# One more step of a linear-attention kernel sends its query and key transposes to the DMA engines

## The chip, the cores and the metric

The kernel runs on one core of a Trainium2 chip. The metric is the device time of one execution in microseconds (us). A core has a matrix engine (TensorE, called PE in the profile; its weight loads are PEld), VectorE (DVE), ScalarE (ACT), GpSimd (POOL), a queue that only issues transfers (SyncE, SP) and 16 DMA engines that move the data. [...]

## The reference

Decayed linear attention over 4 batches, 8 heads, 768 tokens and head width 64, in blocks of 64 tokens with a running state, and then a two-layer feed-forward net on its output (3072 tokens, 512 to 2048 to 512, tanh GELU between the layers):

```python
for b in range(nb):                                   # blocks of 64 tokens
    intra = (qb @ kb.T * Dmask) @ vb                  # decay mask, causal
    inter = (qb * lam_pow) @ kv_state
    out[:, :, sl] = intra + inter
    kv_state = lam_block * kv_state + (kb * rev_pow).T @ vb
x = out.transpose(0, 2, 1, 3).reshape(B * S, H * D)
g = gelu_tanh(x @ w_in)
result = g @ w_out
```

Inputs and the result are float32.

## The kernel before, in words

**Steps.** The attention is cut into 24 steps. A step is one run of 256 tokens and one half of the heads (4 heads): step s is token run s // 2, half s % 2. For each step the kernel

- loads q, k and v of the step, three transfers of 256 KB each (`load_step`, L60; the transfers are issued at L70 on the SP queue);
- scales q by a decay into float16 on DVE (`cast_q`, L282), casts k on ACT (`cast_k`, L295) and scales v on POOL (`scale_v`, L266);
- transposes q and k so that the head width lies on the partitions. Steps 0 to 7 do it on PE, eight 128x128 products with the identity (`stage_t`, L321), and then DVE or ACT copies the result out of PSUM (L325 to L330; for step 7 it is DVE, L330). Steps from `FIRST_DMA_T` = 8 on do it by one DMA transpose from SBUF to SBUF (`transpose_dma`, L303), and `stage_t` returns at once;
- computes the scores S (`scores`, L350), masks them on DVE (`causal`, L360), and computes the key-value product (L385), the masked scores times v (L399) and the state times q (L408) into the two banks OK; ACT copies the attention out as xT (`x_out`, L487); DVE updates the state (`update`, L506) and POOL spreads it into u (L513).

From step 13 on, two steps are joined in a `burst` (L415), in which the same products stand at L350, L436, L450 and L461.

**Dense product.** The feed-forward net is cut into seven groups of tokens. Its work waits as a list of pieces (`filler`); `fill(n)` puts the next n pieces on PE. A piece of the first layer (`mm1`) is a run of products at L561, whose bank of PSUM ACT then empties with a GELU (L565). Pieces of the second layer are the products at L576 and L640. The last two groups use a scheme with fewer products (L739).

**What sets the order.** Nothing is scheduled at run time. `pin` keeps every instruction in program order on its engine, and the lower part of the kernel (L922 to L1124) writes the order out by hand: `R(n, s)` is the scores of step n together with the products of step s, `U(n)` the second state update, `prep(n)` the casts, the transpose and the scaling of step n, and `fill` the dense pieces between them. Loads are issued ahead of their use, at the places where the order says so. All of them, the stores and the DMA transposes stand in the one SP queue.

**Buffers.** All PSUM tiles come from one pool of eight banks, handed out in turn: the ninth tile takes the bank of the first, and PE waits until that one has been emptied. In the stretch that matters later the turn is: six first-layer tiles (call them a to f), two score tiles for step 13, two for step 14, then two O tiles and two K tiles of the burst. So the scores of step 14 take the banks of a and b, O those of c and d, and K those of e and f.

**Around the change.** `prep(7)` stands after `U(5)`, `stage_t(7)` after `prep(8)`. At L1011 step 7's scores come two dense pieces after its PE transpose; the casts of step 9 are queued between the scores and the products (`ahead`). `load_step(10)` is split: its v is issued after the transpose of step 9.

Of the kernel before, what the change touches and what calls it, by code (L numbers as in the profile page):

```python
# [15 lines left out]
def kernel(  # L16
# [19 lines left out]
    NF = DFF // P  # L36
    NC = DM // P
    NSTEP = B * NSB * 2
    FIRST_DMA_T = 8
    PSUM = bass.MemoryType.PSUM  # L40

    const = ctx.enter_context(tc.tile_pool(name="const", bufs=1))
# [17 lines left out]
    def load_step(s, names="qkv"):  # L60
        b, r = divmod(s, 2 * NSB)
        sb, half = divmod(r, 2)
        ts = ld32.setdefault(s, [])
        for nm, src in (("q", q), ("k", k), ("v", v)):
            if nm not in names:
                continue
            t = ld.tile([P, HH, 2, D], FP32, tag=nm + "32", name=f"{nm}32_{s}")
            rows = src[b, half * HH : (half + 1) * HH, sb * SB : (sb + 1) * SB, :]
            queue = nc.scalar if (nm, s) == ("v", 0) else nc.sync
            pin(queue.dma_start(out=t[:].rearrange("p h j d -> p h (j d)"),  # L70
                                in_=rows.rearrange("h (p j) d -> p h (j d)", j=2)))
            ts.append(t)
# [97 lines left out]
    def load_ahead(s):  # L170
        if s < NSTEP:
            load_step(s)
# [83 lines left out]
    def prep_v(s):  # L256
        scale_v(s)
        if s >= 6:
            if s + 3 == FIRST_DMA_T + 2:
                load_step(s + 3, "qk")  # L260
            else:
                load_ahead(s + 3)

    def scale_v(s):
        tv = a16p.tile([P, 2, HH, D], FP16, tag="v16", name=f"v16_{s}")
        pin(nc.gpsimd.tensor_tensor(wide(tv[:]), ld32[s][2][:], decay(dv, s), ALU.mult))  # L266
        a16[s] = a16[s] + (tv,)

    def prep_qk(s):
        cast_qk(s)  # L270
        transpose_dma(s)

    def cast_qk(s):
        cast_q(s)
        cast_k(s)
# [23 lines left out]
    def transpose_dma(s):  # L299
        tqk = whole_qk.pop(s)  # L300
        if s >= FIRST_DMA_T:
            o = qkp.tile([P, 2, 2, 2, P], FP16, tag="qkT", name=f"qkT_{s}")
            pin(nc.sync.dma_start_transpose(out=o[:].rearrange("p a j h t -> p (a j h) t"),  # L303
                                            in_=tqk[:].rearrange("p a j h d -> p (a j h d)")))
            qkT[s] = o
            if s == FIRST_DMA_T + 1:
                load_step(s + 1, "v")

    def stage_t(s):
        if s >= FIRST_DMA_T:  # L310
            return
        tq, tk = a16[s][:2]
        if s < 4:
            Tps = [ps_M.tile([P, 2, 2, P], FP16, tag="M", name=f"Tps{i}") for i in range(2)]
        else:
            Tps = ps_M.tile([P, 2, 2, 2, P], FP16, tag="M", name="Tps")
        for i, t in enumerate((tq, tk)):
            to = Tps[i] if s < 4 else Tps[:, i]
            for hp in range(2):
                for j in range(2):  # L320
                    pin(nc.tensor.transpose(to[:, j, hp, :], t[:, j, 2 * hp : 2 * hp + 2, :],  # L321
                                            ident[:]))
        o = qkp.tile([P, 2, 2, 2, P], FP16, tag="qkT", name=f"qkT_{s}")
        if s < 4:
            pin(nc.scalar.activation(out=o[:, 0], in_=Tps[0][:], func=AF.Copy))  # L325
            pin(nc.vector.tensor_copy(out=o[:, 1], in_=Tps[1][:]))
        elif s in (5, 6, 8):
            pin(nc.scalar.activation(out=o[:], in_=Tps[:], func=AF.Copy))
        else:
            pin(nc.vector.tensor_copy(out=o[:], in_=Tps[:]))  # L330
        qkT[s] = o
# [212 lines left out]
    def queue_group(g, lead=0, per_set=0):  # L544
# [71 lines left out]
        def product(m, p, part=None):  # L616

            st = of_group

            def bank(name):  # L620
                if name not in st:
                    st[name] = ps_M.tile([P, 1 if name == "X" else NP, HE], FP32, tag="M",
                                         name="M" + name[0])
                return st[name]

            if m in (2, 5, 3):
                dst = bank("Y" if m in (5, 3) else "W")[:, p]
            else:
                dst = bank(f"X{p}")[:, 0]
            opens = m == 1 or (m in (2, 5) and p == 0)  # L630
            closes = m in (2, 3, 4)
            a, b = FACTORS[m]
            for i in range(HF) if part is None else range(HF // 2 * part, HF // 2 * part + HF // 2):
                lhsT = g_rows(a, i)[:, p * P : p * P + P]
                if b in W_SUMS:
                    rhs = w_sum16[:, w_slot[b], i, :]
                else:
                    F, E = b
                    rhs = w_out16[:, F * HF + i, E * HE : E * HE + HE]
                pin(nc.tensor.matmul(dst, lhsT, rhs, start=(opens and i == 0),  # L640
                                     stop=(closes and i == HF - 1), skip_group_check=True))
            if part == 0:
                return
            last = p == NP - 1

            def temp(name):
                if name not in st:
                    st[name] = mtp.tile([P, NP, HE], FP32, tag=name, name=name)
                return st[name]

            def out_tile(T):
                if f"o{T}" not in st:
                    st[f"o{T}"] = otp.tile([P, NP, 2, HE], FP32, tag="o32", name=f"o{T}")
                return st[f"o{T}"]

            def copy(to, of):
                pin(nc.scalar.activation(out=to, in_=of, func=AF.Copy))  # L657

            def store(T, ps=slice(0, NP), es=slice(0, 2)):
                r = row0 + T * HN  # L660
                rows = out[r : r + HN, :].rearrange("(p q) (e d) -> q p e d", q=P, e=2)
                o = out_tile(T)

                def send():
                    for i in [slice(i, i + 1) for i in range(ps.start, ps.stop)]:
                        pin(nc.sync.dma_start(out=rows[:, i, es], in_=o[:, i, es, :]))

                if g == 2:
                    kept_stores.append(send)
                else:  # L670
                    send()

            one = slice(p, p + 1)
            if m == 1:
                copy(temp("m1")[:, p], dst)
            elif m == 2 and last:
                pin(nc.vector.tensor_tensor(out_tile(0)[:, :, 0, :], st["W"][:], st["m1"][:], ALU.add))
            elif m == 5 and last:
                copy(temp("q")[:], st["Y"][:])
            elif m == 6:  # L680
                copy(temp("u2")[:, p], dst)
            elif m == 3 and last:
                pin(nc.vector.tensor_tensor(out_tile(0)[:, :, 1, :], st["Y"][:], st["u2"][:], ALU.add))
                store(0)
            elif m == 7 and last_group:
                pin(nc.vector.tensor_tensor(out_tile(1)[:, p, 1, :], dst, st["q"][:, p], ALU.add))
                if last:
                    store(1, one, slice(1, 2))
            elif m == 7:
                copy(temp("u3")[:, p], dst)  # L690
                if last:
                    pin(nc.gpsimd.tensor_tensor(out_tile(1)[:, :, 1, :], st["u3"][:], st["q"][:],  # L692
                                                ALU.add))
            elif m == 4:
                copy(out_tile(1)[:, p, 0, :], dst)
                if last_group:
                    store(1, one, slice(0, 1 if last else 2))
                elif last:
                    store(1)
# [198 lines left out]
    def fill(n):  # L898
        for _ in range(min(n, len(filler))):
            filler.pop(0)()  # L900

    def R(n, s, ahead=None, keep=False):

        if n is not None:
            scores(n)
        if ahead:
            ahead()
        products(n, s)
        if n is not None:
            causal(n)  # L910
        if s is not None and s % 2 == 1:
            g, i = group_of[s // 2]
            if i == len(groups[g]) - 1 and g > 0:
                queue_group(g)
        if n is not None and not keep:
            update(n, 0)
# [91 lines left out]
    stage_t(7)  # L1008
    sum_wout(1, 4, DVE)
    fill(2)  # L1010
    R(7, 6, lambda: prep_qk(9))  # L1011
    store_pair(0)
    U(7)
    scale_v(9)
    fill(2)

    FILL = {8: (2, 0, 0, 0), 9: (1, 2, 1, 2), 10: (0, 1, 1, 3), 11: (0, 1, 1, 3), 12: (0, 2, 1, 3)}
    for n, (a, b, c, d) in FILL.items():
# [41 lines left out]
    cast_qk(16)  # L1060
    load_step(17, "qk")
    transpose_dma(16)
    load_step(17, "v")
    while kept_stores:
# [88 lines left out]
```

## Time and profile before

The median is 198.97 us (three runs, 198.95 to 199.12); the profiled execution has a span of 197.1 us on the instructions' own clock.

| engine | busy, us | share of the span |
|---|---|---|
| PE | 191.5 | 97% |
| PEld | 140.0 | 71% |
| DVE | 151.6 | 77% |
| ACT | 122.2 | 62% |
| POOL | 73.3 | 37% |

| transfer | count | median from issue to landing, us |
|---|---|---|
| load of q, k or v, 256 KB | 24 each | 5.1 to 5.4 |
| DMA transpose of q and k of one step | 16 | 5.1 |
| store of 256 KB | 23 | 4.2 |

The page shows busy time, the span in 40 slices of 4.9 us, the chain of work that ended last, and the costliest groups of instructions. In a timeline a line is: start (us from the start of the span), duration, engine, source line, operation, the tiles it writes and reads, its shape, how many are merged; in square brackets the idle time of the engine before it and who ended it. A merged line can hold several instructions. A landing is the moment at which the last of the 16 DMA engines has reported a transfer done; it is the issue time plus the time that the answer on transfers gives for that one issue.

### The profile page before, as it was taken

Reading aid. Unit: us, or ns where it says so; the run is one execution under the profiler, and the core shown is the slowest. Engines: PE = TensorE matmul, PEld = TensorE weight load, DVE = VectorE, ACT = ScalarE, POOL = GpSimd, SP = SyncE. Lnnn points to the kernel's source line nnn. Section 1 sums busy time; section 2 is a strip of 40 time slices with the busy share of each in tenths; the row PEclk is TensorE's granted clock in tenths of the full one; section 3 lists DMA queues with packets and bytes.
Section 4 is the critical chain, followed back from the end, with each engine's and each line's share of the span. In section 5 each row is a group of like instructions: output and inputs, shape, how many; then the busy total and the mean of one; then the engine's idle time right before and its main releaser. Section 6 shows DMA issues by size and latency. Waiting matters only on the chain.

```text
span 197.1 us, 5915 instructions
## 1 busy us (share of the span) xinstructions
PE 191.5 (97%) x2431; PEld 140.0 (71%) x2431; DVE 151.6 (77%) x297; ACT 122.2 (62%) x249; POOL 73.3 (37%) x85
## 2 busy tenths in 40 slices
PE   8979999999999999999999999999999999999993
PEld 2556544446888888654688764588888888888882
DVE  4797622789999889849999937998668996588620
ACT  3673878357874685686835378844768845779221
POOL 6594123456554841068854517165002030002000
PEclk9999999999999999999999999999999999999999
DMA  6999999999999999999997998400220300030205
GB/s 172 290 324 384 387 387 388 299 287 292 236 216 225 259 343 220 213 266 247 271 268 149 268 328 213 88 4 0 53 85 25 109 6 0 0 110 0 106 19 197
DMA packets 62810, 38.13 MB, mean 193 GB/s; under 512 B 18624, under 2 KB 55744, under 8 KB 62784
## 3 DMA queue, kind: packets, MB, share of 16 engines
q1 hardware_dynamic: 62240, 37.50, 75.0%
q8 instruction: 19, 0.31, 0.6%
q10 hardware_dynamic: 544, 0.26, 0.5%
q14 instruction: 7, 0.06, 0.1%
HBM read 27.26 MB, written 6.29 MB: 170 GB/s over the span
## 4 chain that ended last, share of the span: by engine, by line
PE 89%; SPq 4%; DMA 4%; ACT 0%; issue 0%
PE Hps L561 25%; PE MX L640 18%; PE MY L640 9%; PE HX L739 7%; PE O2ps L576 7%; PE MW L640 4%; DMA wi<-in_moe_w_in_dram 4%; SPq L70 4%; PE HY L739 4%; PE S L350 3%; PE Hps L830 3%; PE HW L739 2%; PE OK L408 2%; PE O L461 1%; PE O L436 1%; PE OK L399 1%
## 5 line engine op out<-in xcount | busy, mean ns | idle before, releaser
L561 PE MATMUL Hps<-xT,w_in 128*128 128x512 f16 (+1 forms) x288 | 50.5, 332 | 0.0
L513 POOL TENSOR_TENSOR u<-t,lumask 128x256 f16<-128x256 f32 x40 | 30.9, 787 | 39.5 <-DVE t L506 25.8
L561 PEld LDWEIGHTS <-w_in 128*128 128x128 f16 x288 | 27.9, 98 | 19.1
L565 ACT ACTIVATE gT<-Hps 128x512 f16<-128x512 f32 x56 | 33.3, 597 | 11.3 <-PE Hps L561 10.8
L360 DVE TENSOR_TENSOR PT<-S,mask 128x512 f16<-128x512 f32 x48 | 30.3, 681 | 7.5 <-PE S L350 7.5
L266 POOL TENSOR_TENSOR v<-v,dv 128x512 f16<-128x512 f32 x24 | 27.7, 1156 | 18.2 <-DMA v<-in_v_dram 14.2
L640 PEld LDWEIGHTS <-gs 128*128 128x128 f16 x320 | 31.2, 98 | 3.6
L640 PEld LDWEIGHTS <-gT 128*128 128x128 f16 x240 | 23.3, 98 | 3.2 <-ACT gT L565 0.2
L640 PE MATMUL MX<-w_sum,gs 128*128 128x256 f16 x160 | 21.4, 273 | 0.0
L282 DVE TENSOR_TENSOR qk<-q,dq 128x512 f16<-128x512 f32 x23 | 18.4, 802 | 1.7 <-DMA q<-in_q_dram 1.7
L692 POOL TENSOR_TENSOR o<-u,q 128x512 f32<-128x512 f32 (+1 forms) x5 | 6.3, 1253 | 35.2 <-ACT u L657 35.2
L295 ACT ACTIVATE qk<-k 128x512 f16<-128x512 f32 x23 | 14.4, 625 | 7.4 <-DMA k<-in_k_dram 7.2
L610 DVE TENSOR_TENSOR gs<-gT 128x1024 f16<-128x1024 f16 (+1 forms) x24 | 16.9, 711 | 1.6 <-ACT gT L565 1.6
L576 PE MATMUL O2ps<-w_out,gT 128*128 128x512 f16 x64 | 14.6, 379 | 0.0
L487 ACT ACTIVATE xT<-OK 128x256 f16<-128x256 f32 x26 | 9.9, 452 | 6.7 <-PE OK L408 6.2
L739 PEld LDWEIGHTS <-ws 128*128 128x128 f16 x128 | 12.5, 97 | 1.8
L657 ACT ACTIVATE u<-MX 128x256 f32<-128x256 f32 x18 | 6.9, 384 | 10.1 <-PE MX L640 10.1
L487 ACT ACTIVATE xT<-O 128x256 f16<-128x256 f32 x22 | 8.0, 459 | 5.3 <-PE O L461 4.5
L576 PEld LDWEIGHTS <-gT 128*128 128x128 f16 x64 | 6.1, 98 | 6.6
L640 PE MATMUL MY<-w_out,gs 128*128 128x256 f16 x80 | 10.7, 273 | 0.0
L350 PEld LDWEIGHTS <-qkT 64*64 64x64 f16 x384 | 6.0, 106 | 6.6 <-issue 3.6
L640 PE MATMUL MX<-w_sum,gT 128*128 128x256 f16 x80 | 10.4, 273 | 0.0
(96 smaller groups left out, 317.3 us busy)
## 6 DMA issues: line engine op xcount, KB each, us to landing
q<-in_q_dram SPq DMA_DIRECT2D x24, 256.0 KB, 5.1
k<-in_k_dram SPq DMA_DIRECT2D x24, 256.0 KB, 5.1
v<-in_v_dram SPq DMA_DIRECT2D x23, 256.0 KB, 5.4
out_dram<-o SPq DMA_DIRECT2D x23, 256.0 KB, 4.2
wo<-in_moe_w_out_dram SPq DMA_DIRECT2D x4, 1024.0 KB, 9.5
wi<-in_moe_w_in_dram SPq DMA_DIRECT2D x4, 512.0 KB, 8.0
wi<-in_moe_w_in_dram SPq DMA_DIRECT2D x2, 1024.0 KB, 12.7
v<-in_v_dram ACTq DMA_DIRECT2D x1, 256.0 KB, 4.2
```

Of the source, the lines that this page charges most:

```text
L266: pin(nc.gpsimd.tensor_tensor(wide(tv[:]), ld32[s][2][:], decay(dv, s), ALU.mult))
L282: pin(q_eng.tensor_tensor(wide(tq), q32[:], decay(dq, s), ALU.mult))
L295: pin(nc.scalar.activation(out=wide(tk), in_=k32[:], func=AF.Copy))
L360: pin(nc.vector.tensor_tensor(t[:, hl].rearrange("p b c d -> p b (c d)"), Sps[:].rearrange("p b c d -> p b (c d)"), mask[:].unsqueeze(1).t ...
L487: pin(nc.scalar.activation(out=d, in_=o, func=AF.Copy))
L513: pin(nc.gpsimd.tensor_tensor(u[:], state[half][:].unsqueeze(2).to_broadcast([P, 2, 2, D]), lumask[:, 2 * half : 2 * half + 2, :].unsqueez ...
L561: pin(nc.tensor.matmul(by_block(Hps[:, i, :]), w_in16[:, c, f * P : (f + 1) * P], x(c), start=(c == 0), stop=(c == NC - 1)))
L565: pin(nc.scalar.activation(out=dst, in_=Hps[:], func=AF.Gelu_apprx_tanh))
L576: pin(nc.tensor.matmul(O2[tau][0][:], gT[:, f % HF, f // HF, tau * P : (tau + 1) * P], w_out16[:, f, :], start=(n == 0), stop=(n == NF - 1)))
L610: pin(nc.vector.tensor_tensor(g_rows(m, i), g_rows(a, i), g_rows(b, i), op))
L640: pin(nc.tensor.matmul(dst, lhsT, rhs, start=(opens and i == 0), stop=(closes and i == HF - 1), skip_group_check=True))
L739: pin(nc.tensor.matmul(dst[:, i, :], w_in_block(a, slice(c, c + 1), slice(f * P, f * P + P))[:, 0], x_block(b, slice(c, c + 1))[:, 0], sta ...
```

## The change

Step 7 moves from the PE transpose to the DMA transpose. To give the transpose time to land, the attention of step 7 moves two dense pieces later: the two pieces that stood after `U(7)` now stand before `R(7, 6)`, and the casts of step 9, which were queued inside `R(7, 6)`, come ahead of them. The loads of step 9 are split like those of step 10 were: q and k first, then the transpose of step 7, then v. One pair of stores of group 3 becomes one store of 512 KB, so that the number of transfers in the queue is as before from there on.

```diff
-    FIRST_DMA_T = 8
+    FIRST_DMA_T = 7
@@ prep_v
-            if s + 3 == FIRST_DMA_T + 2:
+            if s < 8:
                 load_step(s + 3, "qk")
             else:
                 load_ahead(s + 3)
@@ transpose_dma
-            if s == FIRST_DMA_T + 1:
-                load_step(s + 1, "v")
+            if s == 7:
+                load_step(9, "v")
+            elif s == 9:
+                load_step(10, "v")
@@ store
-                    for i in [slice(i, i + 1) for i in range(ps.start, ps.stop)]:
+                    for i in [ps] if (g, T) == (3, 0) else [slice(i, i + 1) for i in range(ps.start, ps.stop)]:
                         pin(nc.sync.dma_start(out=rows[:, i, es], in_=o[:, i, es, :]))
@@ the order
     stage_t(7)
     sum_wout(1, 4, DVE)
     fill(2)
-    R(7, 6, lambda: prep_qk(9))
+    prep_qk(9)
+    fill(2)
+    R(7, 6)
     store_pair(0)
     U(7)
     scale_v(9)
-    fill(2)
```

On the engines' lists this means: PE loses eight transposes and has 16 products of L561 ahead of the scores of step 7 instead of behind its attention; DVE loses one copy; ACT's list goes from three GELUs, the cast of k of step 9, two xT copies and five GELUs to three GELUs, the cast, two GELUs, the two xT copies and three GELUs; POOL's list is the same; SP gains one DMA transpose between k and v of step 9, and has one store fewer later on.

## The prediction

> **What bounds the kernel now.** I read the page first, parts 2 and 4.
>
> ```profile
> PE   8979999999999999999999999999999999999993
> DMA  6999999999999999999997998400220300030205
> PE 89%; SPq 4%; DMA 4%; ACT 0%; issue 0%
> ```
>
> PE is busy in nearly every slice, and the chain that ended last is PE for 89% of the span. So PE time that goes away should come off the end. But the second row is full too: the DMA engines are busy from the start to about slice 24, 118 us. Step 7 lies in this stretch, so I looked next at PE and at SP around it (timelines of the two).
>
> ```profile
> 49.12 1.04 PE L561 MATMUL Hps<-xT,w_in 128*128 128x256 f16 x8
> 49.99 0.61 PE L321 MATMUL Tps<-ident,qk 128*128 128x128 f16 x8
> 50.44 1.91 PE L561 MATMUL Hps<-xT,w_in 128*128 128x256 f16 x16
> 52.28 0.42 PE L350 MATMUL S<-qkT 64*64 64x128 f16 x16
> ...
> 46.40 0.79 SPq L70 DMA_DIRECT2D k<-in_k_dram  x1
> 47.29 1.24 SPq L70 DMA_DIRECT2D v<-in_v_dram  x1
> 48.62 0.90 SPq L70 DMA_DIRECT2D q<-in_q_dram  x1
> 49.61 0.68 SPq L70 DMA_DIRECT2D k<-in_k_dram  x1
> 50.66 2.45 SPq L303 DMA_TRANSPOSE qkT<-qk  x1
> ```
>
> The eight transposes of step 7 take PE from 49.99 to 50.44, where the next product starts: 0.45 us. On SP the loads of step 9 and 10 are issued one behind the other, and the transpose of step 8 takes 2.45 us to issue. Later ones take between 1.31 and 3.42 us there. [...] the transfers land 5 to 6 us after their issue, at a pace of one 256 KB load per 0.8 to 0.9 us (k of step 9: 46.40 + 5.9 = 52.3; k of step 10: 49.61 + 5.2 = 54.8; three loads, 2.5 us).
>
> What a DMA transpose costs there shows in the windows (us; last column GB/s) on the transpose of step 9:
>
> ```profile
> 57.50:58.00 0.50, 0.50 (x7) 0.46 (x5) 0.50 (x2) 0.33 (x1) 0.00 (x0) 1.00 1.25 281
> 58.00:58.50 0.50, 0.50 (x5) 0.20 (x3) 0.50 (x2) 0.50 (x2) 0.00 (x0) 1.00 3.96 117
> 58.50:59.00 0.50, 0.50 (x41) 0.47 (x44) 0.47 (x2) 0.50 (x2) 0.00 (x0) 1.00 0.07 19
> 59.00:59.50 0.50, 0.50 (x32) 0.40 (x17) 0.50 (x2) 0.21 (x2) 0.00 (x0) 1.00 0.08 18
> 59.50:60.00 0.50, 0.50 (x7) 0.46 (x5) 0.50 (x2) 0.50 (x2) 0.00 (x0) 1.00 1.27 290
> ```
>
> Around 290 GB/s before and after, and next to nothing for over a microsecond in the middle: a transpose in a full queue doesn't only take its own packets' time, it leaves a hole behind which everything waits.
>
> Last, who waits for the stream at its end (timelines of POOL, DVE, ACT and PE at 84 to 88 us):
>
> ```profile
> 83.88 1.04 POOL L266 TENSOR_TENSOR v<-v,dv 128x512 f16<-128x512 f32 x1 [6.35 <-DMA v<-in_v_dram]
> 84.63 0.85 DVE L282 TENSOR_TENSOR qk<-q,dq 128x512 f16<-128x512 f32 x1 [0.88 <-DMA q<-in_q_dram]
> 85.48 0.63 ACT L295 ACTIVATE qk<-k 128x512 f16<-128x512 f32 x1 [0.30 <-DMA k<-in_k_dram]
> 86.02 1.76 ACT L565 ACTIVATE gT<-Hps 128x512 f16<-128x512 f32 x3
> 87.77 0.50 PE L450 MATMUL K<-v,qk 64*64 64x64 f16 x32
> ```
>
> v of step 14, q and k of step 16 are waited for the moment they land. Behind the cast of k of step 16 on ACT stand the GELUs of first-layer tiles d, e, f, which end at 87.78; the K products take the banks of e and f and start at 87.77 to 87.83. So PE is just not held up there: the slack of the chain "k of step 16 lands (85.46), cast, three GELUs, K" is below 0.1 us.
>
> [...]
>
> **The change part by part.**
>
> *PE.* Eight transposes less: -0.45 us on the path. The 16 products of L561 only change places with the attention. Step 7's scores are then due at 52.35 - 0.45 + 2 x 0.87 = 53.65.
>
> *DVE.* One copy (0.69 us, L330) less; ACT the same work in another order. DVE isn't on the chain: nothing on the path.
>
> *The new wait of PE for step 7.* k of step 7 is cast until 47.58 on ACT (46.96 + 0.62). SP reaches the transpose at 47.2, waits 0.6 us, issues at about 47.8. The queue is so deep that this pause empties nothing. It lands behind k of step 9 (52.3). The transpose of step 8 landed on most engines about 1 us, on the last 2.5 us, behind the load before it: 53.3 to 54.8 against 53.65 due. I take 53.3, no stall; at worst 1.1 us.
>
> *The DMA stream.* All that comes after is pushed back by what one transpose costs in the queue. From k of step 10 (54.8) to the transpose of step 13 (76.46 + 6.4 = 82.9) are 28.1 us, with 14 loads at 0.9 (12.6), 6 stores at 0.6 (three stores issued from 68.19 land 0.6 apart) (3.6), and six transposes: 11.9 / 6 = 2.0 us each. Bounds: the smallest pieces I find are 0.9 us (steps 14 and 15, one behind the other, about 2 us of packets for the two and no hole) and the largest 2.5 (step 8). I take 2.0.
>
> *Where the push of 2.0 us ends.* Landing and use of each, and slack after the push with PE 0.45 us earlier: transpose of step 8 57.3 at the latest, used 58.6 (-1.1, but the part of its last engine came late by 1.4; about 0); step 9 60.6, used 63.9 (0.8); step 10 65.1, used 68.4 (0.8); step 11 69.2, used 73.8 (2.2); step 12 76.9, used 80.1 (0.7). These hold or nearly. SP doesn't wait for any engine for more than 0.6 us from 51 to 94 us, so nothing gives the push back: it reaches k of step 16 at 87.5. Then the cast ends at 88.1, the three GELUs at 89.8, and K starts at 89.8 instead of 87.8. The transpose of step 14 is pushed from about 86.3 to 88.3, due at 87.4 before, which is the smaller hold (0.9). After that PE and ACT run with the same steps 2.0 us later, while the stream catches up: from 101 to 104 us SP issues nothing. The 0.45 us saved on PE is lost, for PE merely arrives earlier at the wait. Sum: +2.0 us, 201.0.
>
> *The single store and the split loads of step 9*: v of step 9 lands at about 54.5 and isn't needed before the scaling at 55.94; the store (111.85) lies after the tight stretch. Nothing.
>
> **The rivals.**
>
> 1. *The transpose costs the stream only 0.9 us*, the hole coinciding with one that is there. For it: steps 14 and 15. Against: six transposes at 2.0. K then starts 0.9 later: 199.9.
> 2. *The stream isn't what holds PE*: the K banks or the stream give way, and PE keeps its 0.45 us: 198.5. For it: PE shows no idle gap at 87 us today, and the chain runs through PE. Against: three engines wait for that stream, and PE's slack is measured at under 0.1 us. This is the one that ends faster.
> 3. *The push is swallowed, but the chain through k of step 16 stays*: then an earlier PE waits there for the same landing: 199.0, no change.
> 4. *More than the push*: a hole larger than 2.5 us, or a second hold after K (step 16's transpose, landing at 93.1, due at 94.0): 202.0.
>
> **How the numbers follow.** The main case gets 0.57, rival 1 0.13, rival 2 0.15, rival 3 0.10, rival 4 0.05. The forecast is the main case, 201.0. The range takes in cases 1, 3 and 4 with the bounds of the cost (0.9 to 2.5, and up to 0.8 for a stall on top): 198.9 to 202.3; rival 2 is left out. Slower: 0.57 + 0.13 + 0.05 = 0.75; same 0.10; faster 0.15.
>
> **What would show it.** In the changed profile: PE without the 0.45 us at 50; a DMA hole after 53 us for step 7 and the old ones about 2 us later; ACT waiting for k of step 16 over 2 us, until 87 to 88; the first gap of PE ahead of the K products at 87 to 90 us, about 2 us wide, or ahead of step 14's scores; from 104 us on all as before, late. Wrong would be a landing of k of step 16 before 86.5, or no gap in PE before 95 us.

## The result and the profile after

The changed kernel takes 199.70 us (median of four executions, 199.55 to 200.16) against 198.96 (198.90 to 199.12) for the kernel before, measured in turn on one chip: ratio 1.0040, interval 1.0022 to 1.0057. It is slower by 0.74 us. I had forecast slower by 2.0 (201.0): the direction was right and the time lies in the stated range, but the forecast loss was nearly three times the measured one.

The profiled execution is the longest of the four (200.16, span 198.4; the others have spans of 197.8 to 198.0). It is read here, and what only it shows is said. Lines of the source are two or three further down than before. Two measures of PE are used from here on. An idle time in brackets is what the profile draws as a gap; as it draws a product 0.27 us long where the next one follows 0.11 us behind, the gap is shorter than what the wait cost. So I also compare the starts of the scores of each step with those of the kernel before (PE is "late" or "ahead" by the difference), and what PE "loses" is how much that lateness grows. First the page: the busy rows of PE and of the DMA engines, and the chain by engines.

```profile
PE   8979999999998999999999999999999999999993
DMA  6999999999999999999999999410211200020205
PE 81%; DMA 7%; DVE 5%; SPq 4%; issue 1%; ACT 0%; DVEq 0%
```

Apart from the start and the end, PE has one slice below 9 now, the thirteenth (59.5 to 64.5 us). And DVE, which was no part of the chain before, carries 5% of it. The full stretch of DMA is as long as before. Next, timelines of the changed kernel from step 7 to that slice: PE, then SP, then DVE, then PE again.

```profile
49.24 4.53 PE L563 MATMUL Hps<-xT,w_in 128*128 128x256 f16 x40
53.70 0.42 PE L352 MATMUL S<-qkT 64*64 64x128 f16 x16
...
47.70 2.69 SPq L303 DMA_TRANSPOSE qkT<-qk  x1
...
54.16 1.29 DVE L362 TENSOR_TENSOR PT<-S,mask 128x512 f16<-128x512 f32 x2 [1.05 <-PE S L352]
59.86 0.42 DVE L612 TENSOR_TENSOR gs<-gs,gT 128x512 f16<-128x512 f16 x1
...
62.12 0.79 DVE L612 TENSOR_TENSOR gs<-gT,gs 128x512 f16<-128x512 f16 x1
62.83 1.26 DVE L612 TENSOR_TENSOR gs<-gT 128x512 f16<-128x512 f16 x1
...
61.65 0.60 PE L642 MATMUL MY<-w_out,gs 128*128 128x256 f16 x4
62.96 0.61 PE L642 MATMUL MY<-w_out,gs 128*128 128x256 f16 x4 [0.71 <-DVE gs L612]
```

The same mask, the second of these sums and its reader in the kernel before:

```profile
53.06 1.27 DVE L360 TENSOR_TENSOR PT<-S,mask 128x512 f16<-128x512 f32 x2
...
61.73 1.26 DVE L610 TENSOR_TENSOR gs<-gT 128x512 f16<-128x512 f16 x1
...
62.85 1.04 PE L640 MATMUL MX<-w_sum,gs 128*128 128x256 f16 x8
```

The chain of work that ended last, in order of time, shows what this does in that slice of the changed kernel (start, us, what):

```profile
60.20 1.28 DVE PT L362 x2
...
62.20 1.90 DVE gs L612 x2
...
64.14 0.61 PE MX L642 x4
```

The eight transposes are gone from PE, and the scores of step 7 start at 53.70 without a wait; their DMA transpose, issued at 47.70, landed at 53.12. So far all is as forecast. But the mask of step 7 on DVE starts at 54.16 (before: 53.06), because the scores come two pieces later, and DVE sits idle for 1.05 us ahead of it. DVE, which is busy almost without a break from there on, doesn't make that up: two sums of a second-layer group start at 62.12 instead of 61.02 and end at 64.1 instead of 63.0; the last four products of MY wait for the first of them, and the last four of MX for the second (MY and MX are PSUM tiles of the second layer). The starts of each step's scores, after less before, tell what that is worth to PE: step 6 +0.12, step 8 -0.33 (so the 0.45 of the transposes was saved), step 9 +0.87, and the same at every step to 15. One hold (a place where PE has to wait) of 1.2 us at 62 to 64 us has eaten the saving and made the whole loss up to there.

Then the place where I had expected the hold, in timelines of ACT and PE at 86 to 95 us:

```profile
86.32 0.63 ACT L295 ACTIVATE qk<-k 128x512 f16<-128x512 f32 x1 [0.27 <-DMA k<-in_k_dram]
86.86 1.79 ACT L567 ACTIVATE gT<-Hps 128x512 f16<-128x512 f32 x3
88.63 0.50 PE L452 MATMUL K<-v,qk 64*64 64x64 f16 x32
...
95.08 0.42 PE L352 MATMUL S<-qkT 64*64 64x128 f16 x16 [0.20 <-DMA qkT<-qk]
```

k of step 16 landed at 86.30, 0.84 later than before (85.46; the 0.78 in an expectation below is a little too small), and the cast, the three GELUs and K are late by as much. But PE is late by 0.87 already, so K begins with no gap ahead of it: a second hold, of the same size, hidden behind the first. At 95.08 the scores of step 16 waited for their transpose (landed at 95.04), which took PE from +0.87 to +1.26. Its packets spanned 3.6 us here, in the kernel before 2.1. The spans of the other three executions are 0.7 to 0.9 above that of the kernel before, which fits the first hold without this one; no trace of them was kept.

### The profile page after: what moved, and what is told of

The parts are those of the page before. It is cut to its first block, busy times and chain, and to the rows that moved or that the text cites. A ratio compares the mean times of both kernels' runs of the same rounds, so it can differ in the third digit from the quotient of the medians.

```text
span 198.4 us, 5899 instructions
## 1 busy us (share of the span) xinstructions
PE 191.0 (96%) x2421; PEld 139.3 (70%) x2423; DVE 150.7 (76%) x296; ACT 122.2 (62%) x249; POOL 74.0 (37%) x85
## 4 chain that ended last, share of the span: by engine, by line
PE 81%; DMA 7%; DVE 5%; SPq 4%; issue 1%; ACT 0%; DVEq 0%
PE Hps L563 21%; PE MX L642 17%; PE MY L642 8%; PE HX L741 7%; PE O2ps L578 7%; DMA wi<-in_moe_w_in_dram 4%; PE MW L642 4%; SPq L70 4%; PE HY L741 4%; DMA qkT<-qk 3%; PE S L352 3%; PE Hps L832 3%; DVE gs L612 2%; PE HW L741 2%; PE OK L410 1%; DVE PT L362 1%
## 5 line engine op out<-in xcount | busy, mean ns | idle before, releaser
L515 POOL TENSOR_TENSOR u<-t,lumask 128x256 f16<-128x256 f32 x40 | 31.8, 810 | 40.6 <-DVE t L508 26.2
L612 DVE TENSOR_TENSOR gs<-gT 128x1024 f16<-128x1024 f16 (+1 forms) x24 | 17.4, 730 | 1.8 <-ACT gT L567 1.8
```

The source lines that it names most:

```text
L515: pin(nc.gpsimd.tensor_tensor(u[:], state[half][:].unsqueeze(2).to_broadcast([P, 2, 2, D]), lumask[:, 2 * half : 2 * half + 2, :].unsqueez ...
L612: pin(nc.vector.tensor_tensor(g_rows(m, i), g_rows(a, i), g_rows(b, i), op))
```

## The experiments

Two explanations stood against each other. *DVE first*: the later place of the attention makes DVE late, and PE pays at the sums. *Stream first*, the prediction's own: one transpose more pushes all loads, and PE pays at a cast of k. The kernel before was run beside each of them and had medians of 198.94 to 198.99.

### The two halves of the change apart

The order alone: step 7 stays on PE, only its attention moves (against the kernel before).

```diff
-    R(7, 6, lambda: prep_qk(9))
+    prep_qk(9)
+    fill(2)
+    R(7, 6)
@@
-    fill(2)
```

> The order half of the change alone: step 7 is still transposed on PE and copied by DVE, no transfer is added, and its attention stands two dense pieces later. Theory V (the later mask products push DVE's sums for the second layer, and PE waits for these at 62 us): the mask of step 7 starts about 1.3 us later than in the kernel before, the slack there was about 0.4 us, so a PE gap of 0.9 us at 62 to 64 us and 199.9 us in all. Theory D (only the DMA stream holds PE): no transfer is added, so 199.0 us and no gap at 62 us.

Measured: 200.14 (199.97 to 200.59), ratio 1.0045, 1.0031 to 1.0059. Timelines of DVE and of PE:

```profile
54.36 1.29 DVE L360 TENSOR_TENSOR PT<-S,mask 128x512 f16<-128x512 f32 x2 [1.35 <-PE S L350]
...
63.16 0.61 PE L640 MATMUL MY<-w_out,gs 128*128 128x256 f16 x4 [0.71 <-DVE gs L610]
```

The same wait, at the same products, with not one transfer changed. PE is 0.13 ahead at step 8 and 1.06 late from step 9 to the end. So the order alone costs at least as much as the whole change (the intervals of the two ratios overlap): DVE first is right for the hold at 62 us.

The DMA half alone: order and PE transposes as before, the loads, the store and one transpose of step 7 as in the changed kernel; nobody reads what that transpose writes (the part that adds it, shortened):

```diff
+        elif s == 7:
+            o = mtp.tile([P, 2, 2, 2, P], FP16, tag="u3", name="dum0")
+            pin(nc.sync.dma_start_transpose(out=..., in_=tqk...))
+            load_step(9, "v")
```

> The DMA half alone: the order and the PE transposes of the kernel before, and in addition the DMA transpose of step 7 into a buffer that nobody reads, at the place in the queue that the change gives it, with the loads of step 9 split in the same way. Theory D with 2.0 us per transpose (as predicted): k of step 16 lands at 87.5, the K products wait, 201.0 us. Theory D with 0.9 us (a transpose costs its packets[...]): k of step 16 lands at 86.3, PE's first gap is at the K products at 88 us, 199.8 us. Theory V alone: no gap anywhere, 199.0 us.

Measured: 200.34, spread from 199.02 to 201.38; ratio 1.0055, 1.0037 to 1.0073. Timelines of ACT and PE of the profiled execution (199.88):

```profile
80.96 0.63 ACT L295 ACTIVATE qk<-k 128x512 f16<-128x512 f32 x1 [2.27 <-DMA k<-in_k_dram]
81.49 0.36 ACT L663 ACTIVATE u<-MX 128x256 f32<-128x256 f32 x1
...
81.91 1.03 PE L646 MATMUL MX<-w_sum,gT 128*128 128x256 f16 x8 [0.87 <-ACT u L663]
```

The stream does cost PE time, but in this execution, one of the shorter ones, at a place that I hadn't looked at: the cast of k of step 14. It waits for its load, ACT's copy u stands behind it, and MX wants the bank that u empties. PE is on time until step 12 and 0.98 late from step 13 on. Each half alone costs 1 us or more by the medians, both together 0.74: the holds aren't added, since a PE that is late already doesn't wait at the second. This half has the split loads and the joined store in it too; they weren't run without a transpose.

Two unused transposes instead of one doubled the push:

> The same with two such unused transposes, one behind the other. 2.0 us each: k of step 16 lands at 89.5, 203 us. 0.9 us each: lands at 87.2, K products about 1.7 us late, 200.7 us. Theory V alone: 199.0 us.

Measured: 202.10 (200.75 to 202.45). In the profiled execution PE lost 1.15 at the scores of step 8, which waited for their transpose, 0.35 by step 12 and 1.4 at the scores of step 14; it ends 2.96 late. That is three times what one cost in its profiled execution, and only the number of transposes differs. The first had used up the slack, as I read it.

### Which waits are behind which

k of step 16, cast behind the three GELUs and not ahead of them (against the changed kernel; the two loads of step 17 keep their places about the transpose):

```diff
-    cast_qk(16)
+    cast_q(16)
     load_step(17, "qk")
+    scale_v(16)
+    fill(3)
+    cast_k(16)
     transpose_dma(16)
@@
-    scale_v(16)
-    fill(3)
```

> The changed kernel with one edit: ScalarE casts k of step 16 behind the three GELUs whose inputs are ready, not ahead of them. In the changed kernel k of step 16 landed at 86.24 us, 0.78 later than before, and K of step 13 started 0.86 later, but PE was already 0.87 late from the sums at 62 us. Theory 'sums first' (the hold of VectorE at 62 us sets the 0.87; the late k only lies behind it): 199.6 to 199.9, PE still 0.87 late at step 13 and after. Theory 'late k' (the prediction's own: what the pushed stream costs is paid at k of step 16): 198.7 to 199.0, PE back to the earlier kernel's times from step 15 on.

Measured: 199.77 (199.55 to 202.28), as the changed kernel. By the medians, the place that the prediction blamed costs nothing while DVE is late. The profiled execution doesn't serve to see it: it is the longest of the twenty (202.28) and lost 2.3 us at the scores of step 16, which waited for their transpose.

The attention of step 7 one piece later instead of two:

```diff
     prep_qk(9)
-    fill(2)
+    fill(1)
     R(7, 6)
     store_pair(0)
     U(7)
     scale_v(9)
+    fill(1)
```

> The changed kernel with the attention of step 7 one piece of product later instead of two (1.1 us earlier than in the changed kernel). Theory 'the mask of step 7 sets VectorE's time to the sums': the scores are then due at 52.6 and wait for the transpose until 53.1, the mask starts at 53.5 to 53.6, 0.6 earlier than in the changed kernel, and PE's wait at the sums falls from 1.2 to 0.5 or 0.6; the late k of step 16 and the transpose of step 16 then come out as waits of up to 0.5 each: 199.2 to 199.7. Theory 'the place doesn't matter, the pushed stream does': 199.7, the same as the changed kernel, with PE 0.87 late only from step 13 on.

Measured: 200.83 (200.15 to 201.15), slower than both guesses. The trace (of the shortest of four) did what the first theory said up to step 11: PE sat idle 0.24 at the scores of step 7, didn't wait at the sums, and was 0.07 ahead at step 9. Then it lost 1.16 at 82 us behind the cast of k of step 14, as with the DMA half alone. I had listed the wrong next hold.

The transpose of step 16 ahead of q and k of step 17:

```diff
+    transpose_dma(16)
     load_step(17, "qk")
-    transpose_dma(16)
     load_step(17, "v")
```

> The changed kernel with the transpose of step 16 issued ahead of q and k of step 17. Theory 'the scores of step 16 waited for their transpose in the longer executions only' (95.04 landing, scores at 95.08, 0.4 more): the scores at 94.46 wait for nothing, the 0.87 from the sums stays: 199.6 to 199.8, with no execution above 199.9. Theory 'q and k of step 17 take its place': they land 0.9 later, VectorE's scaling of q of step 17 stands ahead of the mask of step 16, and it is 199.8 to 200.5.

Measured: 199.74, two of eleven executions above 199.9. In the profiled one PE is 0.80 late from step 9 to the end, with no wait at step 16.

### Taking DVE's lateness away

First with two edits: q of step 10 scaled on GpSimd, and the group's first sums asked one piece earlier.

```diff
-        q_eng = nc.gpsimd if s == 3 else nc.vector
+        q_eng = nc.gpsimd if s in (3, 10) else nc.vector
@@
-            behind(5, 0, 4, (1, 2))
+            behind(4, 0, 4, (1, 2))
```

> The changed kernel with DVE relieved around the mask of step 7: q of step 10 is scaled on POOL instead of DVE (0.6 us less on DVE), and the first two sums of the second layer of group 1 stand ahead of that mask, in DVE's idle microsecond, instead of behind it. Computes the same. Theory V alone: the gap at 62 us goes, 198.6 us. Theory D with 0.9 us as a second hold behind it: the gap at 62 us goes, but K of the burst then waits for the cast of k of step 16 at 88 us, 199.7 us as the changed kernel. If neither is a hold: 199.7 us with the gap still there.

Measured: 199.80 (199.35 to 201.05). In the profiled execution, one of the longest (200.96), what PE loses at the sums fell from 1.2 to 0.4, and three other losses came up: 0.3 at the scores of step 8, 0.7 at K, 1.1 at the scores of step 16. With k of step 16 cast behind the GELUs as well:

> The changed kernel with two relieved places: VectorE (sums of the group at 62 us asked one piece earlier, q of step 10 scaled on GpSimd) as in the run that relieved VectorE alone, and k of step 16 cast behind the GELUs. Theory 'several holds of one size, one behind the other': the 0.5 us that K waited in the run with VectorE alone goes, and some of the hold at the sums (0.5) and at the transpose of step 16 (0.2 to 1.1) stays: 199.2 to 199.7. Theory 'one hold': 198.5, 0.45 below the kernel before.

Measured: 199.86 (199.43 to 201.42). The wait at K went; PE lost 1.0 at the sums and 0.5 at the scores of step 16 (profiled: 200.00). The next kernel has the two edits on DVE without that of k of step 16. It casts k of step 14 behind the attention of step 12,

```diff
+        elif n == 12:
+            cast_q(n + 2)
         else:
             prep_qk(n + 2)
@@
         R(n, n - 1, keep=n == 8)
+        if n == 12:
+            cast_k(n + 2)
+            transpose_dma(n + 2)
```

and has the transpose of step 16 ahead of the loads of step 17:

> The changed kernel with every hold relieved that a run has shown: q of step 10 scaled on GpSimd, the sums at 62 us asked one piece earlier, k of step 14 cast behind the attention of step 12, k of step 16 behind the GELUs' place as in the changed kernel, the transpose of step 16 ahead of q and k of step 17. Theory 'holds of one size, one behind the other': what is left is some 0.5 us at the sums at 62 us less the 0.45 that PE saves, and perhaps 0.5 at k of step 16: 199.0 to 199.5. Theory 'the push alone sets the end': 199.7 as the changed kernel.

Measured: 199.52 (199.30 to 200.16), with one hold left (profiled: 199.57): PE lost 1.0 at the sums.

Why DVE gained so little shows in the timelines of POOL and DVE of this last kernel:

```profile
58.59 1.22 POOL L282 TENSOR_TENSOR qk<-q,dq 128x512 f16<-128x512 f32 x1
...
58.94 1.15 DVE L612 TENSOR_TENSOR gs<-gs,gT 128x512 f16<-128x512 f16 x1
```

The sum that took 0.42 us in the changed kernel takes 1.15 beside the GpSimd instruction. GpSimd started first and is done at 59.81, the sum at 60.09. The changed kernel has the same two times for sums of this shape: 1.15 us at 57.41, with GpSimd at work from 57.05 to 58.27, and 0.42 at 59.86, with GpSimd idle. The 0.68 us lifted off DVE came back as 0.73 more in that sum. So the next edit takes work out of the chain without another engine: one addition of the same group goes behind the last sum.

```diff
             elif m == 2 and last:
-                pin(nc.vector.tensor_tensor(out_tile(0)[:, :, 0, :], st["W"][:], st["m1"][:], ALU.add))
+                def add_w():
+                    pin(nc.vector.tensor_tensor(...))      # as above
+                late.append(add_w) if g == 1 else add_w()
@@ behind
                 sum_g(i0, i1, ms)
+                if i0 == 4 and ms == (3,):
+                    while late:
+                        late.pop(0)()
```

> The changed kernel with one VectorE instruction of its chain to the sums at 62 us taken out from ahead of them: the addition o<-MW,m of the second group (0.42 us at 61.78) now stands behind the last sum of that group. Theory 'VectorE's lateness sets the hold at 62 us': the sum that the product waits for ends 0.4 earlier, the wait before the product falls by 0.4, and PE is 0.4 to 0.5 late from step 9 on instead of 0.87: 199.2 to 199.5 (if k of step 14 and k of step 16 then come out as waits, up to 199.7). Theory 'the pushed stream sets the end': PE 0.87 late from step 13 or 16 on at the latest, 199.6 to 199.8.

Measured: 200.22 (199.89 to 200.49). Timelines of DVE, PE and ACT:

```profile
61.81 0.42 DVE L612 TENSOR_TENSOR gs<-gT,gs 128x512 f16<-128x512 f16 x1
...
88.15 0.44 PE L452 MATMUL K<-v,qk 64*64 64x64 f16 x31 [0.30 <-ACT gT L567]
95.24 0.42 PE L352 MATMUL S<-qkT 64*64 64x128 f16 x16 [0.91 <-DMA qkT<-qk]
...
86.01 0.63 ACT L295 ACTIVATE qk<-k 128x512 f16<-128x512 f32 x1 [0.94 <-DMA k<-in_k_dram]
```

The loss at the sums is gone but for 0.2 us (the sum not only starts earlier, it takes 0.42 instead of 0.79), and PE is 0.12 ahead of the kernel before from step 9 to step 14. That settles the first hold. And now, with nothing in front of it, the prediction's own hold stands there: ACT idle for k of step 16, GELUs behind the cast, a gap ahead of K that costs PE 0.44, and then 1.1 at the scores of step 16. So the kernel gained nothing: PE runs into the later holds instead. Its median is even 0.5 above that of the changed kernel, but with four executions of each, whose times overlap, I don't call it slower. I had expected 199.2 to 199.7.

### Everything relieved

Edits that had removed a hold, in one kernel: sums and addition as above, k of step 14 later, the transpose of step 16 earlier; q of step 10 is back on DVE, and k of step 16 is where it was.

> All relieved places together: the same addition moved behind the sums, the first sums asked one piece earlier (q of step 10 stays on VectorE, since on GpSimd it ran at 58.59 to 59.81 beside a sum that took 1.15 us instead of 0.42), k of step 14 cast behind the attention of step 12, the transpose of step 16 ahead of q and k of step 17. Theory 'VectorE's lateness': the wait at 62 us, 0.76 with the other places relieved, falls to 0.1 to 0.4, PE is 0 to 0.3 late from step 9 on, and the push may show again at k of step 16: 198.9 to 199.4. Theory 'the pushed stream sets the end': 199.5 and more.

Measured: 199.33 (199.00 to 199.66), ratio 1.0017, 1.0009 to 1.0024. PE is 0.33 ahead of the kernel before from step 8 on, 0.28 at step 13, and 0.40 late from step 15 on. The only gap is at K, and ACT stood idle for 1.18 us ahead of the cast of k of step 16, with the three GELUs behind it on its list (timelines of ACT and PE):

```profile
86.09 0.63 ACT L295 ACTIVATE qk<-k 128x512 f16<-128x512 f32 x1 [1.18 <-DMA k<-in_k_dram]
...
88.23 0.44 PE L452 MATMUL K<-v,qk 64*64 64x64 f16 x31 [0.30 <-ACT gT L567]
```

The last kernel moves that cast behind the GELUs too; the control has the same edits on the kernel before.

> The kernel with all places relieved (addition behind the sums, first sums a piece earlier, k of step 14 behind the attention of step 12, transpose of step 16 ahead of q and k of step 17), and now k of step 16 cast behind the three GELUs as well. In the run without this last edit PE kept its whole 0.33 until 87.5 us and lost 0.67 at K of step 13 only (ScalarE idle 1.18 for k of step 16, three ready GELUs behind it). Theory 'the push of one transpose is paid at the casts of k and nowhere else': PE stays 0.2 to 0.3 ahead of the kernel before to the end: 198.6 to 198.8, faster than both. Theory 'the push shows at the next transfer whatever is reordered': a wait at the scores of step 15 or 16 or at k of step 17, 199.2 to 199.6.

> The same edits put on the kernel before, without the change (step 7 transposed on PE, its attention at its old place), as a control. It has none of the holds that they relieve (PE has no gap over 0.45 us from 40 to 130 us), so all theories expect 198.9 to 199.1; below 198.8 the edits would be worth something without the change, and the gain of the kernel with all places relieved would be theirs.

Measured: 199.18 for the first, from 198.51 to 200.10 (ratio 1.0012, 1.0001 to 1.0023); 199.16 for the control (1.0005, 0.9997 to 1.0013). Five of 22 executions are at 198.51 to 198.75, where the first theory had them and below the fastest of the kernel before in those rounds (198.79). The rest lose it again: in the profiled one (200.02) the wait at K is gone, but PE lost 0.7 at the scores of step 8, waiting for their transpose, 0.4 between steps 10 and 12, and 0.5 at 96 us, where a product waited for the mask of DVE behind a late q of step 17. My reading is that the extra transpose leaves the stream so little slack that an execution meets one late landing or another; only one execution of this kernel was traced. No kernel here has a median below that of the one before.

Three kernels on the way there. The DMA half alone with k of step 14 moved:

> The transposing half alone (the earlier kernel's order and its PE transposes of step 7, with one unused DMA transpose of step 7 added), and ScalarE's cast of k of step 14, with the transpose of step 14 after it, moved behind the attention of step 12. Without the move PE lost 1.09 us at 80.8 to 81.9: a product waited for its bank, the bank for ScalarE's copy u, and that copy stood behind the cast, which waited for k of step 14. Theory 'the pushed stream is paid where a cast stands ahead of a copy on ScalarE': the gap at 81 goes; the push of 0.8 then has the k of step 16 as its next place, where up to 0.8 is lost: 199.0 to 199.8, PE not late before 87 us. Theory 'the push is paid at the end of the stream whatever the casts do': 199.9 to 200.3 as without the move.

Measured: 200.31 (199.05 to 201.29). In the profiled execution (199.85) the gap at 81 us is gone, PE is on time until step 14, and it loses 0.5 at K and 0.4 at the scores of step 16: the push comes out where the prediction had it, once nothing stands in front. But the median is that of the DMA half without the move (200.34), where my second theory had it: over the executions the move gained nothing.

The attention one piece later, with k of step 14 and the transpose of step 16 moved and q of step 10 on GpSimd:

> The attention of step 7 one piece later instead of two, q of step 10 scaled on GpSimd, k of step 14 cast behind the attention of step 12, the transpose of step 16 ahead of q and k of step 17. With one piece alone PE waited 0.51 at the scores of step 7, nothing at the sums at 62 us, and 1.22 at 81 us behind the cast of k of step 14. Theory 'one behind the other': PE on the earlier kernel's times until 87 us, then at most 0.8 at k of step 16: 198.9 to 199.7. Theory 'the push alone sets the end': 200 and more, as with one piece alone.

Measured: 199.41 (199.00 to 201.33; the profiled execution is the longest). And those two moves of step 14 and step 16 on the kernel before:

> The kernel before with the two moves that relieve casts and transposes (k of step 14 cast behind the attention of step 12, the transpose of step 16 ahead of q and k of step 17), as a control: if they are worth something without the change, it is below 198.9. In the kernel before neither place has a wait (k of step 14 is cast at 78.73 with nothing ended by a transfer, the scores of step 16 stand 0.4 behind their transpose), so both theories expect 198.9 to 199.1; more than that would say that the moves cost something themselves.

Measured: 199.13 (ratio 1.0015, 0.9995 to 1.0035). They give nothing by themselves.

## Why the prediction was wrong in size

- **PE, -0.45 us.** Right: 0.45 between the scores of step 6 and step 8; those of step 7 started at 53.70 (forecast 53.65).
- **The transpose of step 7, "I take 53.3, no stall".** Right: it landed at 53.12.
- **"DVE isn't on the chain: nothing on the path".** This step failed: it had the wrong path. I read the chain of the kernel before, in which DVE has no share, and counted the copy that goes. I did not follow the attention two pieces down to the instruction that reads its scores. That instruction heads an ordered list, and the sums for a second-layer group stand 8 us further along it. The trace of the kernel before had the slack: the second sum ended at 61.73 + 1.26 = 62.99, and the four products of MX that read it were due at 62.85 + 4 x 0.11 = 63.29. That is 0.3 us; DVE came 1.1 late, and PE went from -0.33 to 1.1 - 0.3 = +0.8 (measured +0.87, the first hold that PE meets).
- **"I take 2.0" for the push of the stream.** Mis-sized, and this is the term that made the forecast too large: k of step 16 landed 0.84 later. 0.9, the lower bound and rival 1, is the size; with it the prediction's own path would have given 199.9. The 2.0 was a mean over the six transposes of steps 8 to 13, and the packets of every one of these spanned 1.6 to 2.6 us, with a stretch inside of under 40 GB/s; I took such a hole for the transpose's own cost. Windows of the changed kernel on the transposes of step 8 and step 9 (last column GB/s):

```profile
55.50:56.00 0.50, 0.50 (x7) 0.45 (x5) 0.40 (x3) 0.41 (x1) 0.27 (x1) 1.00 1.28 291
59.00:59.50 0.50, 0.50 (x7) 0.46 (x7) 0.50 (x2) 0.41 (x2) 0.00 (x0) 1.00 4.14 99
59.50:60.00 0.50, 0.50 (x7) 0.46 (x5) 0.47 (x2) 0.36 (x2) 0.00 (x0) 1.00 0.07 19
```

  The packets of the transpose of step 8 pass from 55.12 to 56.07 with the rate unbroken (274 GB/s in the half microsecond before the first line). Those of step 9 come in two parts, until 59.32 and from 60.04, and little moves in between. In each of the two traces six transposes up to that of step 13 span over 1.5 us (steps 8 to 13 before; 7 and 9 to 13 after), so one more transpose added its packets, 0.95 us, and no hole.
- **"The slack of the chain k of step 16, cast, three GELUs, K is below 0.1 us".** Right, as a mechanism and in its place: wherever nothing held PE earlier (DMA half with k of step 14 moved, addition deferred, everything relieved but k of step 16) the first gap after 65 us is ahead of K, and PE loses 0.4 to 0.7 us there. In the changed kernel it was hidden behind DVE's hold.
- **"These hold or nearly", the list of transposes of steps 8 to 12.** Too short: it had the transposes and left out the casts of k, which stand in ACT's list ahead of copies that PE needs. k of step 14 is the stream's first hold where DVE isn't late (the DMA half, and the attention one piece later).
- **Rivals.** Rival 1 had nearly the right time, 199.9, and the right push, but put the first hold at K; that the hold at the sums has the same size is luck. Rival 4's second hold, the transpose of step 16, came in the profiled one of the four executions, for 0.4 us. One of the marks that I had named for being wrong came true: k of step 16 landed before 86.5. And PE's first gap was at 62 us, not ahead of K.

## What to carry to other kernels

When work is moved later, follow each engine that reads its result to the end of what is queued behind the reader, even where that engine has no share in the critical chain: it can be off the chain by 0.3 us. Holds on one engine's time are not added: the later one shows only what the earlier one hasn't already cost, so an experiment that removes the first may gain nothing; relieve several before judging one. And price a transfer by what it adds next to a like one, not by a mean over a stretch that has other things in it.

## What the runs showed of the hardware

- The packets of the DMA transposes (256 KB each) spanned, from the start of the first to that of the last, 0.93 to 0.97 us at steps 14 and 15 of the kernel before and at steps 8, 14 and 15 of the changed kernel, 1.6 at step 11 of both, and 2.1 to 3.6 at all others of steps 7 to 17. At step 13 of the kernel before, one of the long ones, they started until 80.24 and again from 81.27, and in between the engines moved 20 GB/s; fifteen of the sixteen parts of q of step 15, a load ahead of it, had landed by 79.55 and the last at 81.01. What makes some of them long was not shown.
- Taking 0.42 us out of VectorE's list ahead of a sum brought the end of that sum 0.68 us forward (from 62.91 to 62.23): it started at 61.81 instead of 62.12 and took 0.42 us instead of 0.79. In the changed kernel a GpSimd instruction had started at 62.01, ahead of the sum; that this made the sum longer there is my reading.
- The executions of each kernel with one transpose more spread over 0.6 to 2.7 us. Of those of the kernel before, measured beside them, about four in five lie within 0.3 us of the fastest, but single ones are up to 2.3 us above it. So medians of a few executions that differ by a few tenths are not told apart.
